# A gated mix of linear attention and a ReLU layer on one core: the kernel without its Block, a work unit on another PSUM bank, and two token tiles loaded as one

## The chip, the cores and the metric

The kernel runs on one core of a Trainium2 chip. The metric is the time of one execution on the device in microseconds; the median of several runs is given, less is better. A profiled execution gives a trace with every instruction of the five engines: TensorE (PE, its weight loads PEld), VectorE (DVE), ScalarE (ACT), GpSimd (POOL) and SyncE (SP), and of the DMA queues. A run's own time is longer than the span of its trace, which reaches from the first to the last instruction of the program.

## The reference

```python
x = A_x                                              # 1 x 2048 x 512, bf16
g = _sigmoid((x * gate_w).sum(-1, keepdims=True))
a = _A_ref(x, A_wqkv, A_w_phi, A_wo)
b = _B_ref(x, B_w1, B_w2)
return g * a + (1 - g) * b

# _A_ref, 32 heads of 16
q, k, v = qkv[0], qkv[1], qkv[2]                     # x @ wqkv, by head
pq = einsum("bhsd,hdf->bhsf", q, w_phi); pk = einsum("bhsd,hdf->bhsf", k, w_phi)
phi_q = concatenate([softmax(pq), softmax(-pq)]); phi_k = concatenate([softmax(pk), softmax(-pk)])
kv = einsum("bhsf,bhsd->bhfd", phi_k, v); z = einsum("bhsf->bhf", phi_k)
o = (phi_q @ kv) / (phi_q @ z + 1e-6)
return o.transpose(0, 2, 1, 3).reshape(B, S, D) @ wo

# _B_ref, hidden size 1376
return relu(x @ w1) @ w2
```

Each output row depends on its own token, and on all tokens only through the sums `kv` and `z`. The order in which tokens stand in the core does not matter as long as each row goes back to its place.

## The kernel before

The 2048 tokens are 16 tiles of 128 (m = 0 to 15) and four chunks of 512 (c = 0 to 3). Everything works on the transposed input XT (features by tokens) and is written out as a graph of named tasks. `ORDER` gives for each engine the order of its tasks by hand; `emit` walks it, puts a wait on a semaphore ahead of each task whose inputs come from another engine or a DMA, and each task raises the semaphore of its engine (each DMA its own).

The start, which the change touches:

- SP issues the loads in the order of `ORDER["sp"]`: token tile 0 (x00), the first and third part of W1 (w1a0, w1a2), token tiles 2 and 3 (x02, x03), the next 512 columns of W1 (w1b), w_phi (wphi), the transposing load of the keys' weights (wkT), the rest of W1 (w1c), the values' weights (wv), and the later ones. ScalarE issues x01, w1a1 and w1a3. Each of the loads x00 to x03 has 128 rows of 1 KB.
- TensorE first runs six matmuls without inputs (`warm0`, L258), then transposes the four tiles of chunk 0 by matmuls against an identity: xt{m}{n} (L350), two blocks each, n = 0, 1; the evictions into XT are xe{m}0 on ScalarE (L362) and xe{m}1 on VectorE (L365). Tile m uses the PSUM banks 0 and 1 (m = 0, 2) or 6 and 7 (m = 1, 3). The first four W1 units run in pieces as tiles and weights come in: hh0 to hh3 (L410), hr0, hr1 and h0_0 to h0_3 (L416), in banks 3, 4, 5 and 2.
- From the fifth unit on, h{c}_{k} is a W1 unit of four 512-column matmuls (L396) for chunk c and hidden tile k. It takes banks 3, 4, 5 in turn and waits until the ReLU that last read the bank, rl{c}_{k} on ScalarE (L474), is done. So h0_4 takes bank 3 after rl0_0, h0_5 bank 4, h0_6 bank 5, h0_7 bank 3 after rl0_4.
- The folds f1_0 to f1_3 (L374) multiply the keys' weights by w_phi in banks 0, 1, 6 and 7, once wkT is there. They are evicted by fe1_0 and fe1_2 on VectorE and fe1_1 and fe1_3 on ScalarE (L344, L342). The first key projection pr_k0 (L510) waits for all four.

Then follow, interleaved by `ORDER`, the W1 units, the values (L490), the key and query features (projections L510, evictions L537, maximum and minimum L541 and L543, subtractions L550, exponential L555, sums L557, normalizations L564 and L587), the sums kv (L571), their product with the queries (L614), and the two output products in one PSUM bank (L636 and L642). oe{m} on ScalarE scales and evicts a tile of the output (L687) and st{m} stores it, 128 rows of 1 KB (L690). The last tile is split by columns (L657, L668), evicted by ScalarE and VectorE and stored by both queues (L681).

At the end SP waits for the stores that nothing else waits for (L707 to L710). All five programs stand in one `nc.Block()`. With it each engine branches into its part and back, and behind it all engines meet: each drains and reports, GpSimd gathers the reports and releases them (the rows of L188). The same meeting stands ahead of the kernel, behind GpSimd's setting of some constants (the rows of L740).

Of the kernel before, what the change touches and what calls it, by code (L numbers as in the profile page):

```python
# [15 lines left out]

ORDER = {
# [4 lines left out]
    ),  # L22
# [5 lines left out]
    ),  # L28
    "act": (
# [119 lines left out]
def bass_gated_mix__linear_kernel_hedgehog__dense_activation_relu__prompt_kernel(  # L149
# [13 lines left out]
    S, D = x2.shape  # L163
# [24 lines left out]
    with ExitStack() as es:  # L188
# [43 lines left out]
        PS = E(nc.psum_tensor("PS", [P, 8, 512], FP32))  # L232
        EPS = 8 * 512

        def ap(t, row, off, dims):
            return bass.AP(tensor=t, offset=off, ap=[[row, P]] + [list(d) for d in dims])

# [49 lines left out]
        def load_x(m, eng, lat):  # L287
            load(f"x0{m}", eng, XN[:, m, :], x0r[:, m, :], dur=0.45, lat=lat)
# [7 lines left out]
        load_w(1, "act", 3.4)  # L296
        load_w(2, "sp", 3.8)
        load_w(3, "act", 3.95)
        load_x(2, "sp", 4.0)
        load_x(3, "sp", 3.9)  # L300
        load("w1b", "sp", W1[:, :, 512:1024], w1r[:, :, 512:1024], dur=0.5, lat=5.0)
        load("wphi", "sp", WPS[:, :, :], A_w_phi.rearrange("(g hl) r c -> (hl r) g c", g=ND), dur=0.5, lat=4.9)
        load_t("wkT", WT[:, ND:2 * ND, :], A_wqkv[:, D:2 * D], (), 4.1, 2.7)
# [50 lines left out]
        for m in range(4):  # L354
            for n in range(2):
                add(f"xt{m}{n}", "pe", lambda q, m=m, n=n: pe_xt(q, m, n),
                    (f"x0{m}", "ident", f"xe{m - 2}{n}" if m > 1 else None), dur=0.2, boost=9000.0 - 10 * m)
            for n, eng in enumerate(("act", "dve")):
                xo = XT[:, 2 * n:2 * n + 2, m * P:(m + 1) * P]
                xi = PS[:, XB[m][n], 0:2 * P].rearrange("p (j t) -> p j t", j=2)  # L360
                if eng == "act":
                    add(f"xe{m}{n}", eng, lambda q, o=xo, i=xi: q.activation(o, i, ACT.Copy), (f"xt{m}{n}",), dur=0.35,  # L362
                        boost=9000.0 - 10 * m)
                else:
                    add(f"xe{m}{n}", eng, lambda q, o=xo, i=xi: q.tensor_copy(o, i), (f"xt{m}{n}",), dur=0.37,  # L365
                        boost=9000.0 - 10 * m)
# [8 lines left out]
                                start=True, stop=True)  # L375
            return last

        for j in range(ND):
            b = FB[j]
            war = [f"xe{2 + j // 2}{j % 2}"]  # L380
            add(f"f1_{j}", "pe", lambda q, j=j, b=b: pe_fold(q, 1, j, b), ("wkT", *wbd, *war), dur=0.24,
                boost=1800.0)
            evict(f"fe1_{j}", ("dve", "act")[j % 2], WP[:, 1, j, :], b, (f"f1_{j}",), boost=1800.0)
        units = []
        for c in range(NC):
            units += [("h", c, k) for k in range(KT - 1)]
# [2 lines left out]
            if c == 2:  # L389
                units += [("f", 0, j) for j in range(ND)]  # L390
        freed = {b: () for b in (*HB, 2)}
        w1of = {k: (() if k < 4 else ("w1b",) if k < 8 else ("w1c",)) for k in range(KT)}

        def pe_h(q, c, k, b):
# [50 lines left out]
            add(f"go{c}", "dve", lambda q, s4=s4: q.reciprocal(OMG[:, s4], EP[:, s4]), (f"gp{c}",), dur=0.15)  # L445

        for n, (kind, a, k) in enumerate(units):
            b = GB4[n] if n < 4 else HB[(n - 4) % len(HB)]
            if kind == "h":
                halved = n < 4  # L450
                deps = [*xof[a], *w1of[k], prev, *freed[b]]
                if k == KT - 1:
                    deps.append("gw")
                    add(f"h{a}_{k}", "pe", lambda q, a=a, b=b: pe_h_tail(q, a, b), deps, dur=0.69)
                    prev = f"h{a}_{k}"
                    hrow = psap(b * 512, [[KREM + 1, 4], [1, KREM]])
                    add(f"rl{a}_{k}", "act", lambda q, a=a, i=hrow: q.activation(
                        HR[:, a % 2, :, 0:KREM], i, ACT.Relu), (prev, f"hx{a - 2}" if a > 1 else None), dur=0.6, boost=RL)
                    add(f"hx{a}", "sp", lambda q, a=a: q.dma_start_transpose(
                        out=HT[:, KT - 1, chunk(a)].rearrange("p (n t) -> p n t", t=P),  # L460
                        in_=HR[:, a % 2, :, :].rearrange("p n k -> p (n k)")),
                        (f"rl{a}_{k}", "hpad"), dur=1.2, lat=1.6, dma=True)
                    add(f"gr{a}", "dve", lambda q, a=a, b=b: q.tensor_scalar(
                        GL[:, 4 * a:4 * a + 4], psap(b * 512 + KREM, [[KREM + 1, 4]]), GATE_LIMIT, -GATE_LIMIT,
                        ALU.min, ALU.max), (prev, f"rl{a}_{k}"), dur=0.2, boost=500.0)
                    freed[b] = (f"rl{a}_{k}", f"gr{a}")
                    gate(a)
                    continue
                add(f"h{a}_{k}", "pe", lambda q, a=a, k=k, b=b, h=halved:
                    pe_h_rest(q, k, (3 if k < 2 else 2) * P, 4 * P, k > 1) if h else pe_h(q, a, k, b),  # L470
                    deps, dur=(0.22 if k < 2 else 0.44) if halved else 0.87,
                    boost=8000.0 if n < 3 else 0.0)
                prev = f"h{a}_{k}"
                add(f"rl{a}_{k}", "act", lambda q, a=a, k=k, b=b: q.activation(  # L474
                    HT[:, k, chunk(a)], PS[:, b, :], ACT.Relu), (prev,), dur=0.6, boost=RL)
                freed[b] = (f"rl{a}_{k}",)
            else:
                deps = ["wqT", *wbd, prev, *freed[b]]
                add(f"f{a}_{k}", "pe", lambda q, a=a, k=k, b=b: pe_fold(q, a, k, b), deps, dur=0.24, boost=1000.0)
                prev = f"f{a}_{k}"  # L480
                evict(f"fe{a}_{k}", FE, WP[:, a, k, :], b, (prev,), boost=1000.0)
                freed[b] = (f"fe{a}_{k}",)


        VLAG = 4
        widths = [2] * (NT // 2 - 1) + [1, 1]
# [28 lines left out]
        for jn, (kind, tiles) in enumerate(jobs):  # L515
# [61 lines left out]
            else:  # L577
# [29 lines left out]
                for m in tiles:  # L607
# [39 lines left out]
                    if m == NT - 1:  # L647
# [40 lines left out]
                        OSB[:, m % NOS, :], PS[:, ab, :], ACT.Copy, scale=OMG[:, m:m + 1]),  # L688
                        (f"a{m}", f"go{m // 4}", f"st{m - NOS}" if m >= NOS else None), dur=0.69)
                    add(f"st{m}", "act", lambda q, m=m: q.dma_start(  # L690
                        out=o2[m * P:(m + 1) * P, :], in_=OSB[:, m % NOS, :]), (f"oe{m}",), dur=0.5, lat=1.5, dma=True)

        for then in ("mx_k0", "mn_k0"):
            g.follow("mk", then)
# [3 lines left out]
        for t in g.tasks.values():  # L698
            if t.dma:
                sems[t.sem] = nc.alloc_semaphore(f"d_{t.name}")  # L700
        block = E(nc.Block())

        @block.sync
        def _(q):
            g.emit("sp", q, order, sems)

            for m in range(NT - NOS - 2, NT - 1):  # L707
                q.wait_ge(sems[f"st{m}"], 16)
            for hf in range(2):
                q.wait_ge(sems[f"st{NT - 1}_{hf}"], 16)  # L710

        @block.gpsimd
        def _(q):
            g.emit("pool", q, order, sems)

        @block.scalar
        def _(q):
            g.emit("act", q, order, sems)

        @block.vector  # L720
        def _(q):
            g.emit("dve", q, order, sems)

        @block.tensor
        def _(q):
            g.emit("pe", q, order, sems)


# [26 lines left out]
```

## Time and profile before

| | us |
|---|---|
| median of three runs | 151.93 (151.83 to 152.18) |
| the profiled execution, own time | 150.82 |
| its span in the trace | 148.9 |
| TensorE busy in it | 144.6 (97%) |
| first key projection starts (pr_k0) | 12.34 |
| last matmuls (L668) | 145.25, for 1.04 |

In timeline rows the first number is the start in us from the span's start, the second the length, then engine, line, operation, output<-input and count; rows of equal kind are merged, and in brackets stands how long the engine was idle before the row and what ended it. An engine's name with a q is its sequencer, where waits, branches and DMA issues run. Matmuls overlap: a 512-column one has a length of 379 ns, while the next begins 0.22 us after it. Some matmul records are missing from a trace.

### The profile page before, as it was taken

The page shows a single profiled execution, that of the slowest core. Times are in us where ns is not written, and L with a number is a line of the kernel's source. Part 1 is how long each engine was busy: PE and PEld are TensorE (multiplying, and loading weights), DVE is VectorE, ACT ScalarE, POOL GpSimd, SP SyncE. Part 2 cuts the span into 40 slices and gives each one's busy share as a digit, 9 for nine tenths or more (in the row PEclk, how much of TensorE's full clock was granted, in tenths as well). Part 3 has the DMA queues.
Part 4 walks back from the last instruction along what each step waited for, and adds up shares of the span by engine and source line. Part 5 has one row for each costly group of instructions (what it writes and reads, how often), then busy time and mean ns, then how long its engine had stood idle before and what let it go on. Part 6 is the DMA issues. An engine that isn't in the chain of part 4 may idle for free.

```text
span 148.9 us, 2614 instructions
## 1 busy us (share of the span) xinstructions
PE 144.6 (97%) x992; PEld 75.3 (51%) x1009; DVE 111.0 (74%) x168; ACT 91.9 (62%) x127; POOL 109.6 (74%) x72
## 2 busy tenths in 40 slices
PE   7999999999999999999999999999999999999992
PEld 2874444445654475445444554455544454455461
DVE  2532667999896948989999997999999969436301
ACT  3457769799969767898983927366565551310151
POOL 4000599999999999999999999999999791240000
DMA  4999999920030001000000191649677585966552
GB/s 149 302 205 190 220 215 193 349 71 4 12 61 0 0 4 37 0 4 0 0 0 0 36 147 35 141 106 142 153 160 198 128 213 106 143 171 146 51 167 69
DMA packets 46364, 16.11 MB, mean 108 GB/s; under 512 B 39856, under 2 KB 46352, under 8 KB 46352
## 3 DMA queue, kind: packets, MB, share of 16 engines
q1 hardware_dynamic: 43616, 13.50, 43.5%
q10 hardware_dynamic: 2736, 2.45, 5.3%
q8 instruction: 8, 0.13, 0.4%
q14 instruction: 4, 0.03, 0.1%
HBM read 4.41 MB, written 2.10 MB: 44 GB/s over the span
## 4 chain that ended last, share of the span: by engine, by line
PE 96%; ACT 1%; issue 1%; DVE 0%
PE PS L636 24%; PE PS L396 21%; PE PS L510 18%; PE PS L490 9%; PE PS L642 9%; PE PS L571 3%; PE PS L614 3%; PE PS L404 2%; PE PS L258 2%; PE PS L657 2%; PE PS L410 1%; PE PS L374 1%; PE PS L350 1%; ACT HT L474 1%; PE PS L668 1%
## 5 line engine op out<-in xcount | busy, mean ns | idle before, releaser
L550 POOL TENSOR_TENSOR TS<-PB,MX 128x1024 bf16<-128x1024 bf16 (+1 forms) x18 | 30.9, 1722 | 14.3 <-DVE MX L541 14.3
L557 DVE TENSOR_REDUCE ZB<-FT 128x128 f32<-128x2048 bf16 (+1 forms) x18 | 36.6, 2032 | 1.8 <-ACT FT L555 1.8
L636 PE MATMUL PS<-W,HT 128*128 128x512 bf16 (+1 forms) x160 | 37.5, 379 | 0.3
L555 ACT ACTIVATE FT<-TS 128x2048 bf16<-128x2048 bf16 (+1 forms) x18 | 30.9, 1718 | 8.7 <-POOL TS L550 8.5
L396 PE MATMUL PS<-XT,W 128*128 128x512 bf16 x141 | 34.3, 379 | 0.2
L550 POOL TENSOR_TENSOR TS<-MN,PB 128x1024 bf16<-128x1024 bf16 (+1 forms) x18 | 30.9, 1724 | 0.8 <-DVE MN L543 0.8
L510 PE MATMUL PS<-WP,XT 128*128 128x512 bf16 x124 | 29.9, 379 | 0.2
L564 POOL TENSOR_TENSOR FT<-FT,SC 128x2048 bf16<-128x2048 bf16 (+1 forms) x9 | 29.5, 3288 | 0.0
L474 ACT ACTIVATE HT<-PS 128x512 bf16<-128x512 f32 x40 | 22.6, 597 | 5.5 <-PE PS L396 4.6
L636 PEld LDWEIGHTS PS<-W,HT 128*128 128x128 bf16 (+1 forms) x165 | 15.5, 98 | 17.1
L541 DVE TENSOR_REDUCE MX<-PB 128x64 bf16<-128x1024 bf16 (+1 forms) x18 | 19.5, 1085 | 6.0 <-ACT PB L537 6.0
L687 ACT ACTIVATE OSB<-PS,OMG 128x512 bf16<-128x512 f32 x15 | 10.2, 687 | 22.3 <-PE PS L642 22.2
L543 DVE TENSOR_REDUCE MN<-PB 128x64 bf16<-128x1024 bf16 (+1 forms) x18 | 19.3, 1084 | 3.2 <-ACT PB L537 3.2
L396 PEld LDWEIGHTS PS<-XT,W 128*128 128x128 bf16 x144 | 13.8, 98 | 15.3
L537 ACT ACTIVATE PB<-PS 128x1024 bf16<-128x1024 f32 (+1 forms) x18 | 16.7, 927 | 6.8 <-PE PS L510 3.7
L510 PEld LDWEIGHTS PS<-WP,XT 128*128 128x128 bf16 x128 | 12.0, 98 | 13.6 <-DVE WP L344 0.4
L587 POOL TENSOR_TENSOR FT<-FT,SR 128x1024 bf16<-128x1024 bf16 (+1 forms) x9 | 15.6, 1739 | 0.7
L490 PE MATMUL PS<-WV,XT 128*128 128x512 bf16 x61 | 15.8, 379 | 0.2
L642 PE MATMUL PS<-WO,OT 128*128 128x512 bf16 x58 | 14.3, 379 | 0.1
L623 DVE SCALAR_TENSOR_TENSOR OTM<-PS,EG,RD 128x256 bf16<-128x256 f32 x32 | 13.8, 463 | 0.4 <-DVE RD L621 0.2
L621 DVE RECIPROCAL RD<-PS 128x16 f32<-128x16 f32 x32 | 6.4, 232 | 8.9 <-PE PS L614 8.7
L499 ACT ACTIVATE VS<-PS 128x512 bf16<-128x512 f32 x16 | 9.6, 602 | 4.3 <-PE PS L490 4.3
(54 smaller groups left out, 104.9 us busy)
## 6 DMA issues: line engine op xcount, KB each, us to landing
out_dram<-OSB ACTq DMA_DIRECT2D x15, 128.0 KB, 2.1
W<-in_B_w_dram SPq DMA_DIRECT2D x1, 1280.0 KB, 7.0
W<-in_B_w_dram SPq DMA_DIRECT2D x1, 512.0 KB, 5.1
WV<-in_A_wqkv_dram SPq DMA_DIRECT2D x1, 512.0 KB, 4.5
WO<-in_A_wo_dram SPq DMA_DIRECT2D x1, 512.0 KB, 7.4
FT<-in_A_x_dram SPq DMA_DIRECT2D x3, 128.0 KB, 3.7
W<-in_B_w_dram SPq DMA_DIRECT2D x1, 352.0 KB, 3.7
W<-in_B_w_dram ACTq DMA_DIRECT2D x2, 128.0 KB, 3.5
```

What stands on the lines that cost most here:

```text
L396: last = q.matmul(PS[:, b, :], W1[:, j, k * P:(k + 1) * P], XT[:, j, chunk(c)], start=(j == 0), stop=(j == ND - 1))
L474: add(f"rl{a}_{k}", "act", lambda q, a=a, k=k, b=b: q.activation(HT[:, k, chunk(a)], PS[:, b, :], ACT.Relu), (prev,), dur=0.6, boost=RL)
L490: last = q.matmul(PS[:, 2, :], XT[:, j, m * P:(m + 1) * P], WV[:, j, :], start=(j == 0), stop=(j == ND - 1))
L510: last = q.matmul(PS[:, n, :], XT[:, j, m * P:(m + 1) * P], WP[:, s, j, :], start=(j == 0), stop=(j == ND - 1))
L541: add(f"mx_{J}", "dve", lambda q, sl=sl, w=w, i=pbg: q.tensor_reduce(MX[:, sl, 0:w * H], i, AX.X, ALU.max), (f"ev_{J}", old("t1")), dur=0. ...
L543: add(f"mn_{J}", "dve", lambda q, sl=sl, w=w, i=pbg: q.tensor_reduce(MN[:, sl, 0:w * H], i, AX.X, ALU.min), (f"ev_{J}", old("t2")), dur=0. ...
L550: add(f"{tn}_{J}", "pool", lambda q, o3=o3, a3=a3, b3=b3: q.tensor_tensor(o3, a3, b3, ALU.subtract), (f"{'mx' if sg == 0 else 'mn'}_{J}", ...
L555: add(f"ex_{J}", "act", lambda q, fs=fs, ts=ts, w=w: q.activation(FT[:, fs, 0:w * F], TS[:, ts, 0:w * F], ACT.Exp), (f"t1_{J}", f"t2_{J}", ...
L557: add(f"sm_{J}", "dve", lambda q, fs=fs, sl=sl, w=w: q.tensor_reduce(ZB[:, sl, 0:2 * w * H], FT[:, fs, 0:w * F].rearrange("p (g d) -> p g ...
L564: add(f"nm_{J}", "pool", lambda q, f3=f3, sl=sl, w=w: q.tensor_tensor(f3, f3, SC[:, sl, 0:2 * w * H].unsqueeze(2).to_broadcast([P, 2 * w * ...
L636: last = q.matmul(PS[:, ab, :], HT[0:r, k, m * P:(m + 1) * P], W2[0:r, k, :], start=(k == 0), stop=False)
L642: last = q.matmul(PS[:, ab, :], OT[:, m % NOT, t, :], WO[:, t, :], start=False, stop=(t == ND - 1))
```

## The change

- The Block goes: the five programs are emitted one after the other into the main program, and SP's last waits stand behind them. No branches and no meeting of the engines remain at the end; the one ahead of the kernel stays.
- The loads x02 and x03 become one load x0b: partition p gets the rows 256+2p and 257+2p of x, which lie behind each other in memory, as one packet of 2 KB. So tile 2 holds the even and tile 3 the odd rows of the 256. All eight transposes of the two tiles wait for x0b. Their output rows go back to every second row (`stored`).
- h0_4 takes bank 6 (FB[2]) instead of bank 3 and so waits for xe30, the eviction of tile 3's first half from this bank, and not for rl0_0. f1_2, which uses bank 6 next, waits for rl0_4 as well as for xe30 (written xe{2 + j // 2}{j % 2}). h0_7 in bank 3 then waits for rl0_0.
- ScalarE does rl0_4 ahead of fe1_1 and fe1_3 instead of behind them and rl0_5.

TensorE's order and VectorE's and GpSimd's are as before.

```diff
 "sp":
-        "x00 w1a0 w1a2 x02 x03 w1b wphi wkT w1c wv x1 x2 wqT x3 ...
+        "x00 w1a0 w1a2 x0b w1b wphi wkT w1c wv x1 x2 wqT x3 ...
 "act":
-        "x01 w1a1 w1a3 xe00 xe10 xe20 xe30 rl0_0 rl0_1 rl0_3 rl0_2 fe1_1 fe1_3 rl0_5 rl0_4 ev_k0 rl0_8 rl0_6 "
+        "x01 w1a1 w1a3 xe00 xe10 xe20 xe30 rl0_0 rl0_1 rl0_3 rl0_2 rl0_4 fe1_1 fe1_3 rl0_5 ev_k0 rl0_8 rl0_6 "
...
+        def stored(m):
+            if m in (2, 3):
+                return o2[2 * P:4 * P, :].rearrange("(p n) d -> p n d", n=2)[:, m - 2, :]
+            return o2[m * P:(m + 1) * P, :]
...
-        load_x(2, "sp", 4.0)
-        load_x(3, "sp", 3.9)
+        load("x0b", "sp", FT[:, NF - 2, 2 * D:4 * D], x2[2 * P:4 * P, :].rearrange("(p m) d -> p (m d)", m=2),
+             dur=0.45, lat=3.9)
...
             add(f"xt{m}{n}", "pe", lambda q, m=m, n=n: pe_xt(q, m, n),
-                    (f"x0{m}", "ident", f"xe{m - 2}{n}" if m > 1 else None), dur=0.2, boost=9000.0 - 10 * m)
+                    (f"x0{m}" if m < 2 else "x0b", "ident", f"xe{m - 2}{n}" if m > 1 else None), dur=0.2, boost=9000.0 - 10 * m)
...
+        freed[FB[2]] = ("xe30",)
...
-            b = GB4[n] if n < 4 else HB[(n - 4) % len(HB)]
+            b = GB4[n] if n < 4 else FB[2] if n == 4 else HB[(n - 4) % len(HB)]
...
+            war = [f"xe{2 + j // 2}{j % 2}"] + (["rl0_4"] if j == 2 else [])
...
-                        out=o2[m * P:(m + 1) * P, :], in_=OSB[:, m % NOS, :]), (f"oe{m}",), dur=0.5, lat=1.5, dma=True)
+                        out=stored(m), in_=OSB[:, m % NOS, :]), (f"oe{m}",), dur=0.5, lat=1.5, dma=True)
...
-        block = E(nc.Block())
-
-        @block.sync
-        def _(q):
-            g.emit("sp", q, order, sems)
...
+        for e, q in (("sp", nc.sync), ("pool", nc.gpsimd), ("act", nc.scalar), ("dve", nc.vector), ("pe", nc.tensor)):
+            g.emit(e, q, order, sems)
+
+        for m in range(NT - NOS - 2, NT - 1):
+            nc.sync.wait_ge(sems[f"st{m}"], 16)
+        for hf in range(2):
+            nc.sync.wait_ge(sems[f"st{NT - 1}_{hf}"], 16)
```

More of the change, by code (lines that the diff above doesn't have):

```diff
@@ L376, in pe_fold @@
             return last
[L378 to L383, printed above, removed]
         units = []
@@ L482, in bass_gated_mix__linear_kernel_hedgehog__dense_activation_relu__prompt_kernel @@
                 freed[b] = (f"fe{a}_{k}",)
+        for j in range(ND):
+            b = FB[j]
+            war = [f"xe{2 + j // 2}{j % 2}"] + (["rl0_4"] if j == 2 else [])
+            add(f"f1_{j}", "pe", lambda q, j=j, b=b: pe_fold(q, 1, j, b), ("wkT", *wbd, *war), dur=0.24,
+                boost=1800.0)
+            evict(f"fe1_{j}", ("dve", "act")[j % 2], WP[:, 1, j, :], b, (f"f1_{j}",), boost=1800.0)
         VLAG = 4
@@ L700, in bass_gated_mix__linear_kernel_hedgehog__dense_activation_relu__prompt_kernel @@
                 sems[t.sem] = nc.alloc_semaphore(f"d_{t.name}")
-        block = E(nc.Block())
-        @block.sync
-        def _(q):
-            g.emit("sp", q, order, sems)
[L707 to L726, printed above, removed]
+        for e, q in (("sp", nc.sync), ("pool", nc.gpsimd), ("act", nc.scalar), ("dve", nc.vector), ("pe", nc.tensor)):
[4 more added lines that the diff above has]
+            nc.sync.wait_ge(sems[f"st{NT - 1}_{hf}"], 16)
 _INS = ['A_x', 'A_wqkv', 'A_w_phi', 'A_wo', 'B_x', 'B_w1', 'B_w2', 'gate_w']
```

2 rows, old and new, of the table ORDER are left out of this document.

## The prediction

> **What bounds the kernel now.** I read the page first, then the chain that ended last, then the stages and the start and the end instruction by instruction.
>
> ```profile
> span 148.9 us, 2614 instructions
> PE 144.6 (97%) x992; PEld 75.3 (51%) x1009; DVE 111.0 (74%) x168; ACT 91.9 (62%) x127; POOL 109.6 (74%) x72
> PE 96%; ACT 1%; issue 1%; DVE 0%
> ```
>
> The third line is the chain by engine: from the first matmul to the last the time is TensorE's. The table by stage says where TensorE is not simply busy (stretch, length, then busy time and instructions of PE, PEld, DVE, ACT, POOL, clock, DMA):
>
> ```profile
> 12.34:143.00 130.66, 129.81 (x872) 65.70 (x888) 105.33 (x152) 83.85 (x113) 107.92 (x63) 1.00 0.47 97
> 146.32:148.90 2.58, 0.00 (x0) 0.00 (x0) 0.38 (x1) 0.28 (x1) 0.00 (x0) 1.00 0.17 51
> ```
>
> Between 12.34 and 143 TensorE has 0.85 us without a record in 130.66, at clock 1.00. No instruction of that stretch changes, so it can only move as a block. The change can act before 12.34, where loads still decide, and after 146.32, where 2.58 us pass with no matmul.
>
> **The start, as it is.** TensorE's rows around token tiles 2 and 3 and the fifth W1 unit (start, length):
>
> ```profile
> 5.63 0.38 PE L410 MATMUL PS<-XT,W 128*128 128x256 bf16 x2
> 5.95 0.23 PEld L350 LDWEIGHTS PS<-IDN,FT 128*128 128x128 bf16 x4 [0.21 <-DMA FT<-in_A_x_dram]
> 6.30 0.23 PEld L350 LDWEIGHTS PS<-IDN,FT 128*128 128x128 bf16 x4
> 6.54 0.60 PE L410 MATMUL PS<-XT,W 128*128 128x256 bf16 x4
> 8.63 0.42 PEld L396 LDWEIGHTS PS<-XT,W 128*128 128x128 bf16 x3
> 8.96 1.67 PE L396 MATMUL PS<-XT,W 128*128 128x512 bf16 x7
> ```
>
> Four 256-column matmuls take 0.60 of which the last 0.27 is its own length, so they start 0.11 apart; the one before the wait starts at 5.63+0.11=5.74 and leaves TensorE free at 5.85. It goes on at 5.95 (load x02, 0.10 lost), does four transposes in 0.23, and goes on again at 6.30 (load x03, 0.12 lost). The rest of the start runs without a gap until 8.96.
>
> There the chain of waits leaves TensorE for ScalarE:
>
> ```profile
> 7.84 1.09 ACT HT L474 x2
> ```
>
> That would be the fifth unit, h0_4, waiting for rl0_0 to free bank 3. It is a missing record (the page has 992 matmuls to 1009 weight loads): two units are eight matmuls and seven are shown, while the weight loads begin at 8.63 and go on one matmul ahead. 8.96 is the second matmul of h0_4, 0.22 after an unrecorded one at 8.74. h0_4 does not wait for a bank.
>
> **Part 1: the Block goes.** At the end (one row per instruction: duration three times, then first and last start):
>
> ```profile
> L710 SPq EVENT_SEMAPHORE  x2: 28/28/28, 148.3 to 148.5; - x2
> L188 PEldq DRAIN  x1: 1757/1757/1757, 144.6 to 144.6; - x1
> L188 SPq COMPARE_BRANCH  x1: 33/33/33, 148.6 to 148.6; - x1
> L188 SPq DRAIN  x1: 7/7/7, 148.7 to 148.7; - x1
> L188 POOLq EVENT_SEMAPHORE  x2: 17/17/17, 148.8 to 148.8; - x2
> L188 PEldq EVENT_SEMAPHORE  x1: 51/51/51, 148.9 to 148.9; - x1
> ```
>
> SP's wait for the last store ends at 148.5. Then come a branch, a drain, GpSimd's gathering and release, and every engine's passing of it, until 148.9: 0.4 us in series behind the last store, and nothing hides it. All of it goes, so the span ends with the wait at 148.5: **-0.4 us**. The other drains lie under SP's wait already and give nothing.
>
> Outside the span lie 150.82-148.9=1.9 us of the profiled run. No row shows them. Today all engines leave the kernel together at 148.9; then the other four would leave before SP, TensorE by 4 us (its drain at 144.6), and closing work that they must do one after another could lie under SP's wait. The nearest rows for how far apart engines come when no barrier holds them are the opening ones:
>
> ```profile
> L740 SPq DRAIN  x1: 7/7/7, 0.0 to 0.0; - x1
> ...
> L740 PEldq DRAIN  x1: 8/8/8, 0.3 to 0.3; - x1
> ...
> L740 SPq EVENT_SEMAPHORE  x1: 17/17/17, 0.7 to 0.7; - x1
> ```
>
> ```profile
> 0.74 0.40 SPq L272 DMA_DIRECT2D FT<-in_A_x_dram  x1
> ...
> 2.13 0.91 SPq L272 DMA_DIRECT2D FT<-in_A_x_dram  x2
> ```
>
> 0.3 us between the first and the last. Bounds 0 and -0.3; a loss I exclude, since no engine arrives later than today. I take the middle, **-0.15**. At the entry the branches have no row; between SP's release (0.7 above) and its first load (0.74, in SP's timeline) lie some 0.05 us, so they cost between 0 and 0.05: **-0.03**, and it shifts loads and warm-up matmuls alike.
>
> **Part 2: x02 and x03 become x0b.** From the page the queues (packets, MB, share of 16 engines' span) and the landings (count, KB each, us from issue to landing):
>
> ```profile
> q1 hardware_dynamic: 43616, 13.50, 43.5%
> q10 hardware_dynamic: 2736, 2.45, 5.3%
> ...
> W<-in_B_w_dram SPq DMA_DIRECT2D x1, 512.0 KB, 5.1
> ...
> FT<-in_A_x_dram SPq DMA_DIRECT2D x3, 128.0 KB, 3.7
> ```
>
> x0b is issued at 2.13 (SP's timeline above), where x02 was. Its first half is no longer usable before its second. How long do 2 KB packets take? q10: 5.3% of 16x148.9 us over 2736 packets is 46 ns for 895 bytes on the mean; q1: 43.5% over 43616 is 23.8 ns for 310 bytes. That is 0.038 ns a byte and 12 ns a packet: estimated 51 ns for 1 KB and 90 for 2 KB. Each of 16 engines moves 8 of the 128 packets: 8x(2x51-90)=0.10 us saved. So I let x0b release TensorE 0.10 before x03 did, at 6.20. Eight transposes take 2x0.235=0.47 (four and the step to the next group are 6.54-6.30=0.24), the next matmuls (hh3) start at 6.67 instead of 6.54: **+0.13**. Even is a release at 6.07.
>
> The rule that speaks against the joining is in the Trainium skill, "DMA: Bandwidth & Descriptors", section "Why a DMA increments its semaphore by 16 and not by 1": only the full 16, one from each engine, means that the data is there. The trace agrees (two loads, two releases, 5.95 and 6.30); by it the joined load costs tile 2 the 0.25 between 5.95 and my 6.20.
>
> Bounds of the release: not before TensorE is free at 5.85, -0.22 (both gaps); and by size between the 3.7 us of 128 KB and the 5.1 us of 512 KB, a third of the way up, 4.2 us: landing at 6.3, release 6.4, +0.33. I take +0.13, nearest x03's own row, since the same engines move the same bytes.
>
> The evictions of both tiles come right behind:
>
> ```profile
> 6.27 0.74 ACT L362 ACTIVATE XT<-PS 128x256 bf16<-128x256 f32 x2 [1.61 <-PE PS L350]
> 6.38 0.78 DVE L365 CAST XT<-PS 128x256 bf16<-128x256 f32 x2 [1.47 <-PE PS L350]
> 6.97 1.93 PE L416 MATMUL PS<-XT,W 128*128 128x128 bf16 x24
> ```
>
> VectorE's first cast (half of the 0.78 and a little, 0.43) ends at 6.81, 0.86 after the first transpose. TensorE wants it at 6.97 now, 1.02 after; without the pause between the tiles it comes 0.47+0.43=0.90 after, with its weight load a little sooner: 0 to 0.05, **+0.02**.
>
> SP issues one load fewer, some 0.45 us; w1b, wphi and wkT are issued that much sooner. That buys nothing as long as TensorE comes later than before. The stride of tiles 2 and 3 on the way out keeps 128 rows of 1 KB, and
>
> ```profile
> ACT OSB L687 <- PE PS L642: 22.2, 12, 8.3
> ```
>
> the evictions behind those stores wait 22.2 us for TensorE, not for stores: 0. Uncovered, a store's landing of 2 us would stand before an eviction.
>
> **Part 3: h0_4 to bank 6.** It loses a wait on rl0_0 that was over (above): 0. In exchange f1_2 waits for rl0_4, which ScalarE now does ahead of fe1_1:
>
> ```profile
> 7.84 2.18 ACT L474 ACTIVATE HT<-PS 128x512 bf16<-128x512 f32 x4 [0.83 <-PE PS L416]
> 10.37 0.98 PEld L374 LDWEIGHTS PS<-WBD,WT 128*128 128x128 bf16 x16 [0.23 <-DMA WT<-in_A_wqkv_dram]
> 11.12 1.08 ACT L342 ACTIVATE WP<-PS 128x512 bf16<-128x512 f32 x2 [1.09 <-PE PS L374]
> 12.31 0.13 PEld L510 LDWEIGHTS PS<-WP,XT 128*128 128x128 bf16 x2 [0.42 <-DVE WP L344]
> ```
>
> ScalarE is done with four rl at 10.02; a fifth of 0.6 ends at 10.6. f1_2 loads half-way through 0.98 from 10.37, at 10.86, and fe1_1 starts at 11.12: it fits in ScalarE's 1.09 idle with 0.26 to spare, and all of it shifts with TensorE. Cost 0; were rl0_4 later by x, f1_2, f1_3, fe1_2 and pr_k0 (12.31) would be later by x-0.26.
>
> **Sum:** -0.4-0.15-0.03+0.13+0.02 = -0.43 us; the profiled run's 150.82 becomes 150.4. The three timed runs have a median of 151.93, 1.1 above the profiled run; I carry the difference over: **151.5 us**.
>
> **The rivals.**
> - *The front gains as well.* x0b releases before 5.85, and the 0.22 of gaps goes. For it: one issue and half the packets. Against: the 128 KB loads took 3.7 us at this place, queued behind 768 KB. wkT then stops part of it: the fold's weight load waited until 10.37 with a matmul slot at 10.47, so 0.1 passes unless wkT comes earlier too, which its earlier issue speaks for. Price: 151.93-0.58-0.22=151.1. The Trainium skill's same page, "Anatomy of one DMA", has a fit (for the other, software path) of 2.0 us plus bytes over 436 GB/s: 2.6 us for 256 KB, a landing at 4.7 and this result. For 128 KB it gives 2.3, and the rows say 3.7, so I do not believe it here.
> - *The end gains nothing.* What follows the span joins the engines at the same hour anyway, and only the front is left: 151.93+0.15-0.03=152.05. For it: 1.9 us outside the span that I cannot see. Against: the last store is SP's alone to wait for, and the 0.4 lies in series behind it. That is the case in which the change doesn't do what it says.
> - *Slower: x0b is late.* One slow DMA engine holds all eight transposes, where today tile 2 can go ahead. At the 512 KB load's 5.1 us it would land at 7.23; hh3 starts at 7.75, 1.2 later, and 151.93-0.58+1.2=152.55. It decides from a release of 6.07+0.58=6.65 on. Against: twice the bytes of x02, not four times.
>
> **How the numbers follow.** A change of 0.2% is 0.30 us, about what can be told from none, so 151.63 to 152.23 is "no change". The forecast 0.58, the front gaining 0.14, the end not gaining 0.18, x0b late 0.10. The forecast's own bounds are 150.95 (-0.4-0.3-0.05-0.22) and 151.9 (-0.4+0.38); some 0.05 of its chance lies above 151.63. Faster 0.53+0.14=0.67; no change 0.05+0.17=0.22; slower 0.11. Range 150.95 to 152.05: it takes in the gaining front and the end that gains nothing, and leaves out the late load and the outermost corners.
>
> **What would show it.** The span's last row is SP's wait, with no branch, drain or gathering behind it, and the time outside the span is 1.6 to 1.9 us. One group of eight transposes starts near 6.2 with one wait, hh3 near 6.65. h0_4's weight loads follow on without a gap and the fold shows no wait for ScalarE. The stretch from the first pr_k0 matmul to the last keeps its 130.7 us. Wrong it is if x0b's release lies outside 5.85 to 6.5, if the time outside the span grows by what the span loses, or if waits on ScalarE or GpSimd appear between 13 and 143.

## The result, and the profile after

| | before | changed |
|---|---|---|
| median of 22 runs each, us | 151.55 (150.74 to 152.40) | 150.99 (150.33 to 151.67) |
| the profiled execution, own time | 150.82 | 151.05 |
| its span | 148.9 | 149.4 |
| time outside the span, mean over the runs (before: its 86 runs beside the experiments) | 1.86 | 1.61 |

The ratio is 0.9962, 95% interval 0.9947 to 0.9977: the change makes the kernel 0.56 us faster, about 0.4%. A second comparison of the same two kernels (e5 below) gave 150.91 beside 151.18, ratio 0.9978 (0.9958 to 0.9998). Two of its twelve runs, 152.77 and 152.98, were in a slower state and are left out here and below. Forecast was -0.43 us.

The two profiled executions tell the opposite at first sight, since the span after is 0.5 us *longer*. The page and the table by stage of the changed kernel:

```profile
span 149.4 us, 2618 instructions
PE 145.6 (97%) x1009; PEld 74.9 (50%) x1009; DVE 110.8 (74%) x168; ACT 91.7 (61%) x127; POOL 109.5 (73%) x72
...
12.34:143.00 130.66, 130.66 (x888) 65.36 (x885) 106.05 (x154) 84.03 (x114) 107.87 (x63) 1.00 0.46 97
```

This time no matmul record is missing (1009 to 1009 weight loads), and TensorE is busy through all of 12.34 to 143: the 0.85 us without a record before were missing records and no wait. The difference lies at the two edges. First the end; the group of SP's last waits of the changed kernel (last two numbers: first and last start):

```profile
L714 SPq EVENT_SEMAPHORE  x2: 28/28/28, 149.2 to 149.4; - x2
```

It is the last row of the span. The branch, the drain and the gathering that followed it for 0.4 us before are gone. Now the start, TensorE's weight loads in the timeline of the changed kernel:

```profile
4.99 0.21 PEld L410 LDWEIGHTS PS<-XT,W 128*128 128x128 bf16 x2
6.20 0.34 PEld L410 LDWEIGHTS PS<-XT,W 128*128 128x128 bf16 x4 [1.01 <-issue]
6.84 0.45 PEld L355 LDWEIGHTS PS<-IDN,FT 128*128 128x128 bf16 x8 [0.29 <-DMA FT<-in_A_x_dram]
7.25 0.37 PEld L410 LDWEIGHTS PS<-XT,W 128*128 128x128 bf16 x4
7.82 1.67 PEld L416 LDWEIGHTS PS<-XT,W 128*128 128x128 bf16 x24 [0.20 <-ACT XT L367]
9.51 1.50 PEld L396 LDWEIGHTS PS<-XT,W 128*128 128x128 bf16 x8
11.13 1.10 PEld L379 LDWEIGHTS PS<-WBD,WT 128*128 128x128 bf16 x16
12.18 0.58 PEld L396 LDWEIGHTS PS<-XT,W 128*128 128x128 bf16 x4
13.19 0.13 PEld L517 LDWEIGHTS PS<-WP,XT 128*128 128x128 bf16 x2 [0.42 <-DVE WP L349]
```

All eight transposes stand in one group with one wait, as forecast, but at 6.84 and not at 6.20, and ahead of them TensorE waits 1.01 us. What it waits for there is in the waits of the changed kernel (us in total, times, longest):

```profile
PE PS L410 <- DMA W<-in_B_w_dram: 0.8, 1, 0.8
```

A quarter of W1 (w1a2, which hh2 needs ahead of tile 2) was late: it landed 4.4 us after its issue, and 3.3 us before. The change does not touch this load. That the larger packets behind it hold it up is not shown: it took 3.6 to 4.4 us in the six profiles with the joined load, and 3.3 to 4.4 in the seven with two loads. pr_k0 starts at 13.19, 0.88 after the 12.31 of before, and the end gives 0.4 back: that is the longer span. Is 0.9 us the price of the joined load? One execution can't say: the spans of the changed kernel's runs alone reach from 148.7 to 150.0 us. The experiments show that this start was an unlucky one, and that of the profile before a lucky one. The start makes most of the spread: from pr_k0's first weight load to the span's end pass 136.1 to 136.4 us in every profile without the Block.

### The profile page after: what moved, and what is told of

Same layout as the page of the kernel before. It is cut to its first block, busy times and chain, and to the rows that moved or that the text cites. A ratio compares the mean times of both kernels' runs of the same rounds, so it can differ in the third digit from the quotient of the medians.

```text
span 149.4 us, 2618 instructions
## 1 busy us (share of the span) xinstructions
PE 145.6 (97%) x1009; PEld 74.9 (50%) x1009; DVE 110.8 (74%) x168; ACT 91.7 (61%) x127; POOL 109.5 (73%) x72
## 4 chain that ended last, share of the span: by engine, by line
PE 94%; DMA 3%; SPq 1%; DVE 0%; issue 0%
PE PS L643 24%; PE PS L396 21%; PE PS L517 19%; PE PS L497 9%; PE PS L649 9%; DMA W<-in_B_w_dram 3%; PE PS L578 3%; PE PS L621 3%; PE PS L404 2%; PE PS L664 2%; PE PS L416 1%; PE PS L379 1%; PE PS L410 1%; PE PS L675 1%; SPq L277 1%; PE PS L355 0%
## 5 line engine op out<-in xcount | busy, mean ns | idle before, releaser
L643 PE MATMUL PS<-W,HT 128*128 128x512 bf16 (+1 forms) x165 | 38.1, 379 | 0.0
L517 PE MATMUL PS<-WP,XT 128*128 128x512 bf16 x128 | 30.6, 379 | 0.0
L497 PE MATMUL PS<-WV,XT 128*128 128x512 bf16 x64 | 16.4, 379 | 0.0
```

Source lines behind the costliest of these rows:

```text
L497: last = q.matmul(PS[:, 2, :], XT[:, j, m * P:(m + 1) * P], WV[:, j, :], start=(j == 0), stop=(j == ND - 1))
L517: last = q.matmul(PS[:, n, :], XT[:, j, m * P:(m + 1) * P], WP[:, s, j, :], start=(j == 0), stop=(j == ND - 1))
L643: last = q.matmul(PS[:, ab, :], HT[0:r, k, m * P:(m + 1) * P], W2[0:r, k, :], start=(k == 0), stop=False)
```

## The experiments

Each kernel was timed beside runs of the kernel before, in lots: e1 to e4 (median before 151.47), e5 to e8 (151.18), e9 to e11 (151.22), e12 (151.39). In the table "span" is the mean span less that of the lot's runs of before, with its 95% bound; "outside" is the mean of time less span; tile 2 and pr_k0 are the starts of their first weight load in the one profiled execution. Kernel before: outside 1.84 to 1.89, tile 2 5.95, pr_k0 12.31.

| | what it is | median | ratio, 95% | span | outside | tile 2 | pr_k0 |
|---|---|---|---|---|---|---|---|
| e1 | no Block alone | 150.25 | 0.9926, 0.9897 to 0.9955 | -0.65±0.33 | 1.33 | 6.29 | 12.71 |
| e6 | the same again | 150.25 | 0.9946, 0.9926 to 0.9966 | -0.35±0.26 | 1.33 | 6.50 | 13.07 |
| e2 | joined load alone | 151.30 | 0.9988, 0.9971 to 1.0005 | -0.22±0.17 | 1.85 | 6.46 | 13.03 |
| e3 | bank and order alone | 151.38 | 0.9988, 0.9972 to 1.0004 | -0.15±0.20 | 1.84 | 6.61 | 13.05 |
| e4 | no Block, bank, order | 150.45 | 0.9935, 0.9910 to 0.9959 | -0.50±0.26 | 1.32 | 6.28 | 12.70 |
| e5 | changed kernel again | 150.91 | 0.9978, 0.9958 to 0.9998 | -0.09±0.23 | 1.61 | 6.71 | 13.05 |
| e7 | e1, waiting for both loads | 150.78 | 0.9971, 0.9947 to 0.9996 | -0.03±0.29 | 1.37 | 6.98 | 13.34 |
| e8 | changed, rl0_4 late | 151.86 | 1.0044, 1.0024 to 1.0065 | +0.87±0.23 | 1.60 | 6.39 | 14.04 |
| e10 | changed, one wait more | 150.49 | 0.9949, 0.9929 to 0.9969 | -0.22±0.22 | 1.33 | 6.55 | 12.89 |
| e11 | e1, permuted rows | 150.31 | 0.9931, 0.9909 to 0.9953 | -0.37±0.30 | 1.35 | 6.43 | 13.25 |
| e12 | changed, two waits more | 150.57 | 0.9948, 0.9922 to 0.9973 | -0.27±0.30 | 1.32 | 6.43 | 12.87 |

### e1 and e6: only the Block goes

```diff
-        block = E(nc.Block())
-        @block.sync
...
+        for e, q in (("sp", nc.sync), ("pool", nc.gpsimd), ("act", nc.scalar), ("dve", nc.vector), ("pe", nc.tensor)):
+            g.emit(e, q, order, sems)
+        for m in range(NT - NOS - 2, NT - 1):
+            nc.sync.wait_ge(sems[f"st{m}"], 16)
```

> The kernel before with nothing changed but the Block taken away. Forecast of the prediction: -0.4 us in the span, about -0.15 outside it (the first chip result suggests up to -0.27: 1.92 us lay outside the span before, 1.65 after), nothing at the entry: -0.55 to -0.7 us, a ratio of 0.9955 to 0.9965. Rival 'only what the span shows': -0.4 us, 0.9973, with 1.9 us outside the span. Rival 'the end gains nothing': 1.000, the span shorter and the time outside it longer by the same 0.4.

> The kernel without the Block alone, as the partner of the run above: 0.992 to 0.994 against before. Span some 0.45 us shorter than before's, time outside it some 0.5 us shorter. If the -0.5 outside the span belonged to one chip only, it falls to the 0.3 of the first result: 0.995.

Both lots gave 150.25 us, 1.2 and 0.9 us below their runs of before, and about 0.7 below the changed kernel. From the last weight load on TensorE to the span's end pass 2.53 us in e1 and 2.93 to 2.96 in the kernels with the Block; the last row is SP's wait again:

```profile
L707 SPq EVENT_SEMAPHORE  x2: 28/28/28, 148.6 to 148.8; - x2
```

That is the 0.4 us inside the span. Outside it the kernel gains a further 0.53 us (1.86 to 1.33), three and a half times what the prediction gave it and twice what the changed kernel has. The gain forecast for e1 (0.9955 to 0.9965) was too small for that reason. So the changed kernel loses half of that gain again, and something in its start too.

### e2: only the joined load

```diff
-        load_x(2, "sp", 4.0)
-        load_x(3, "sp", 3.9)
+        load("x0b", "sp", FT[:, NF - 2, 2 * D:4 * D], x2[2 * P:4 * P, :].rearrange("(p m) d -> p (m d)", m=2),
```

> The kernel before with x02 and x03 joined to x0b, Block and banks as before. Forecast: +0.13 to +0.15 us, 1.001. Rival 'the front gains as well': -0.22 us, 0.9985. Rival 'the joined load is late': +0.5 us and more, 1.003 or above. In the trace one wait ahead of eight transposes.

No difference in time that the runs can tell: 0.9988, and 1.85 us outside, as before. The forecast of 1.001 lies just outside the interval, and the value is nearer to the rival in which the front gains (0.9985): the mean span is 0.22 us shorter, not longer. With the Block the joined load costs nothing outside the span. In its profile:

```profile
6.46 0.45 PEld L355 LDWEIGHTS PS<-IDN,FT 128*128 128x128 bf16 x8 [0.61 <-DMA FT<-in_A_x_dram]
...
11.16 0.90 PEld L379 LDWEIGHTS PS<-WBD,WT 128*128 128x128 bf16 x16 [0.54 <-DMA WT<-in_A_wqkv_dram]
```

The transposes waited 0.61 us for x0b, and the folds waited for wkT, although SP had issued wkT sooner than before. The earlier issue of the later loads bought nothing.

### e3 and e4: the bank and ScalarE's order, with the Block and without

```diff
+        freed[FB[2]] = ("xe30",)
-            b = GB4[n] if n < 4 else HB[(n - 4) % len(HB)]
+            b = GB4[n] if n < 4 else FB[2] if n == 4 else HB[(n - 4) % len(HB)]
-            war = [f"xe{2 + j // 2}{j % 2}"]
+            war = [f"xe{2 + j // 2}{j % 2}"] + (["rl0_4"] if j == 2 else [])
```

> The kernel before with h0_4 in bank 6 and rl0_4 ahead of fe1_1, nothing else. Forecast: 0, ratio 1.000, since h0_4 waited for nothing and ScalarE has 0.26 us to spare for f1_2. Rival 'the 1.1 us on ScalarE in the chain is a wait': -0.2 us or more, 0.9985 or below. Rival 'the fold waits for rl0_4': +0.2 us or more, and a wait for ScalarE at TensorE's L379 or its like.

> The changed kernel with the two loads x02 and x03 of before. If the joined load costs 0.13 us: 0.13 us less than the changed kernel, -0.7 us against before, 0.9953. If it gains 0.22: 0.22 more than the changed kernel, -0.36, 0.9976. If the parts add up, the same as without the Block alone.

0.9988 alone, and without the Block 0.9935 beside the 0.9926 and 0.9946 of e1 and e6: the moved bank gains and costs nothing that can be measured.

### e5, e7: the changed kernel again, and two loads that are both awaited

```diff
-                    (f"x0{m}", "ident", f"xe{m - 2}{n}" if m > 1 else None), dur=0.2, boost=9000.0 - 10 * m)
+                    (*((f"x0{m}",) if m < 2 else ("x02", "x03")), "ident", f"xe{m - 2}{n}" if m > 1 else None), ...
```

> The changed kernel once more, beside the kernel without the Block alone on the same chip. The first comparisons leave 0.4 us between the two (0.9962 and 0.9926), with 1.61 us outside the span for the one and 1.33 for the other, though the rows behind the last store are alike. If that is the chip, both have the same time outside the span here and differ by the joined load alone: forecast +0.13 us against no Block, that is 0.994 to 0.9955 against before. Rival 'the joined load costs more without the Block': 0.996 again, 0.4 us behind.

> No Block; x02 and x03 stay two loads of 1 KB packets, but all eight transposes wait for both. It takes the joint waiting without the 2 KB packets. If the joint waiting is what costs and the packets give 0.10 us back: +0.23 us against no Block alone, +0.10 against the changed kernel. Rival 'the packets give nothing': the same as the changed kernel. Rival 'the wait is on w1a2 and w1a3 anyway, ahead of it': the same as no Block alone.

e5 and e6 ran on one chip, and 1.61 and 1.33 us outside the span came again: that difference belongs to the kernels and not to the chip. The forecast for e5 (0.994 to 0.9955), which took them to be equal there, missed.

e7 has no Block and the two loads of before, but no transpose of either tile begins before both are there. Beside e6 in the same lot its median is 0.5 us higher (0.9971 against 0.9946) and its mean span 0.32±0.36 us longer. That points the way of the forecast (+0.23, since tile 2 may not go ahead) but is not clear of the noise; beside the changed kernel (e5) the mean span is 0.06 us longer. Its rows:

```profile
6.98 0.46 PEld L350 LDWEIGHTS PS<-IDN,FT 128*128 128x128 bf16 x8 [0.42 <-DMA FT<-in_A_x_dram]
7.40 0.37 PEld L410 LDWEIGHTS PS<-XT,W 128*128 128x128 bf16 x4
7.97 1.68 PEld L416 LDWEIGHTS PS<-XT,W 128*128 128x128 bf16 x24 [0.20 <-ACT XT L362]
```

Here too TensorE comes to a stop behind hh3, ahead of the group of 24 (hr0 is its first), as in the changed kernel at 7.82. Which eviction does hr0 wait for? VectorE's casts, of the changed kernel and of e7:

```profile
7.28 0.76 DVE L370 CAST XT<-PS 128x256 bf16<-128x256 f32 x2 [2.45 <-PE PS L355]
```

```profile
7.43 0.76 DVE L365 CAST XT<-PS 128x256 bf16<-128x256 f32 x2 [2.62 <-PE PS L350]
```

And of e1, its weight loads and its casts:

```profile
7.34 1.68 PEld L416 LDWEIGHTS PS<-XT,W 128*128 128x128 bf16 x24
```

```profile
6.80 0.76 DVE L365 CAST XT<-PS 128x256 bf16<-128x256 f32 x2 [2.18 <-PE PS L350]
```

The group of 24 begins 7.82-7.28=0.54 us after the first cast's start here, 7.97-7.43=0.54 in e7, 7.34-6.80=0.54 in e1, and 6.93-6.38=0.55 before, where the prediction saw no wait. A distance that stays the same, whatever else moved, points to a wait, although the profile puts it down to ScalarE: 0.42 for the cast of tile 2 and 0.12 until the weight load goes; hr0 needs tile 2's two evictions alone. It is 0.54 or 0.55 in twelve of the thirteen profiles. The cast begins 0.44 after tile 2's first transpose in both kernels (7.28-6.84, 6.38-5.95). So the start hangs on **tile 2**, already before the change, and the rest follows at a fixed distance: from the group of 24 to pr_k0 it is 5.37 after and 5.38 before.

The thirteenth is e11 (two loads, below). There x03 landed late, at 7.19, and the group of 24 follows behind hh3 without a stop, 0.86 after the cast of tile 2, which began at 6.94:

```profile
7.23 0.23 PEld L356 LDWEIGHTS PS<-IDN,FT 128*128 128x128 bf16 x4 [0.51 <-DMA FT<-in_A_x_dram]
7.42 0.37 PEld L416 LDWEIGHTS PS<-XT,W 128*128 128x128 bf16 x4
7.80 1.75 PEld L422 LDWEIGHTS PS<-XT,W 128*128 128x128 bf16 x24
```

So the second of two loads can decide as well, when it is late enough. And tile 2 does not always start at its load's release. In e6 x02 landed at 5.33 and the last quarter of W1 at 5.17, yet tile 2's first transpose came at 6.50. TensorE was busy until then with the pieces of W1, at half its pace. Its L410 rows between 4.9 and 7, of the kernel before and of e6 (ns, shortest/median/longest; first and last start):

```profile
L410 PE MATMUL PS<-XT,W x17: 219/272/314, 4.6 to 6.9; 128*128 128x256 bf16 x12, 128*128 128x128 bf16 x5
```

```profile
L410 PE MATMUL PS<-XT,W x11: 314/421/421, 4.7 to 6.5; 128*128 128x256 bf16 x8, 128*128 128x128 bf16 x3
```

In e6 the 256-column matmuls start 0.21 us apart, before 0.11. e3 and e12 keep the slow pace beyond 6.0 too; in the other ten profiles it ends between 3.5 and 5.7. The granted clock shown for this stretch of e6 is 1.00, so its rows do not say why. The scatter of the start thus comes from loads and from TensorE's own early pace.

### e8: the cover of rl0_4 taken away

```diff
-  "... rl0_2 rl0_4 fe1_1 fe1_3 rl0_5 ..."
+  "... rl0_2 fe1_1 rl0_4 fe1_3 rl0_5 ..."
```

> The changed kernel with rl0_4 behind fe1_1 instead of ahead of it on ScalarE: the cover of the fold's new wait is taken away. fe1_1 starts 0.75 us after the fold's first weight load and lasts 0.5, rl0_4 another 0.6: f1_2 starts some 1.3 us later than in the changed kernel, and TensorE with it: +1.3 us, 1.005 against before. Rival 'the fold's eviction or wkT is waited for anyway': less than +0.3 us.

In the changed kernel ScalarE's rows around the fold are

```profile
8.72 2.67 ACT L474 ACTIVATE HT<-PS 128x512 bf16<-128x512 f32 x5 [0.89 <-PE PS L416]
11.99 1.08 ACT L347 ACTIVATE WP<-PS 128x512 bf16<-128x512 f32 x2 [0.60 <-PE PS L379]
```

The fifth rl ends at 11.39, and f1_2, the ninth of the sixteen weight loads from 11.13, comes at 11.73: 0.34 us to spare; 0.26 was forecast. In e8 that cover is gone:

```profile
10.67 0.65 PEld L379 LDWEIGHTS PS<-WBD,WT 128*128 128x128 bf16 x8
12.67 0.45 PEld L379 LDWEIGHTS PS<-WBD,WT 128*128 128x128 bf16 x8 [1.35 <-ACT HT L474]
...
14.04 0.34 PEld L517 LDWEIGHTS PS<-WP,XT 128*128 128x128 bf16 x3 [0.38 <-DVE WP L349]
```

TensorE waits 1.35 us for ScalarE between f1_1 and f1_2. The mean span is 0.96 us above that of e5 in the same lot and the median time 0.95; the profile alone would say 1.3 (from tile 2's first transpose to pr_k0 it is 7.65 in e8 and 6.35 in the changed kernel). The edit that costs nothing costs about a microsecond when one task stands one place later.

### e9: the loads by themselves

This kernel leaves the whole computation out and only loads and copies rows of x.

```diff
+        for r in range(8):
+            sp.dma_start(out=X[:, 2:4, :], in_=x2[2 * P:4 * P, :].rearrange("(p m) d -> p m d", m=2)).then_inc(j, 16)
+            sp.wait_ge(j, 16)
+            sp.dma_start(out=X[:, 4, :], in_=x2[4 * P:5 * P, :]).then_inc(a, 16)
+            sp.dma_start(out=X[:, 5, :], in_=x2[5 * P:6 * P, :]).then_inc(b, 16)
+            sp.wait_ge(a, 16)
+            sp.wait_ge(b, 16)
```

> This kernel leaves the whole computation out: SP loads rows of A_x and stores a copy of them, nothing else runs, so only its rows are read and not its time. Eight times it loads 256 KB of two neighbouring rows to a partition (packets of 2 KB, line 34) and waits, then loads two times 128 KB (packets of 1 KB, lines 37 and 38) and waits for both; after that come loads in bulk. Theory (the joined load costs and gains next to nothing, as the estimate of 51 ns for a 1 KB packet and 90 ns for one of 2 KB had it): the median packet of 2 KB takes 80 to 95 ns and that of 1 KB 43 to 53 ns, and the joined load is complete 0.0 to 0.3 us before the second load of the pair counted from the first issue of each, and after the first load of the pair by 0.1 to 0.5 us. Rival one (larger packets move clearly more): a 2 KB packet under 75 ns, and the joined load at least 0.4 us ahead of the pair's second. Rival two (larger packets are worse): a 2 KB packet over 105 ns, and the joined load behind the pair's second.

SP's issues in its timeline: L34 is the joined load, L37 and L38 the pair, and each group is issued when the one ahead is complete.

```profile
6.08 0.33 SPq L34 DMA_DIRECT2D X<-in_A_x_dram  x1
8.61 0.33 SPq L37 DMA_DIRECT2D X<-in_A_x_dram  x1
8.98 0.43 SPq L38 DMA_DIRECT2D X<-in_A_x_dram  x1
11.26 0.33 SPq L34 DMA_DIRECT2D X<-in_A_x_dram  x1
```

The joined load takes 8.61-6.08=2.53 us here and the pair 2.65. From the issue to the landing of the last byte the eight joined loads have a median of 2.60 and the pairs of 2.54, so they are even; the first load of a pair is there at 2.05, half a microsecond ahead of either. The median packet took 84 ns for 2 KB and 46 ns for 1 KB, near the estimates of 90 and 51, but single packets took up to 587 and 307 ns, and the means are 110 and 53. The forecast that the joined load would be a little ahead of the pair's second missed by a hair; both rivals fall on the packets. With these means the prediction's sum for the saving, 8x(2x51-90)=0.10 us, becomes 8x(2x53-110)=-0.03: the larger packets save nothing. The fit in the Trainium skill, "DMA: Bandwidth & Descriptors", section "Anatomy of one DMA", made there for the software path, gives an estimate of 2.6 us for 256 KB: the 2.60 of a load alone, as here, agree. Its estimate of 2.3 for 128 KB is above the 2.05 measured.

In the kernel, behind 768 KB, it is another matter. The page of the changed kernel (count, KB each, us from issue to landing):

```profile
FT<-in_A_x_dram SPq DMA_DIRECT2D x1, 256.0 KB, 4.7
```

### e10, e11, e12: where half of the gain outside the span went

The time outside is 1.61 us in the changed kernel and 1.33 without the Block and with two loads; with the Block it is the same with one load or two. No row shows it.

```diff
+        nc.sync.wait_ge(sems["x0b"], 16)
         for m in range(NT - NOS - 2, NT - 1):
             nc.sync.wait_ge(sems[f"st{m}"], 16)
```

> The changed kernel with one more wait in SyncE's program, ahead of the five last ones, on the joined load, which landed 130 us earlier: it waits for nothing. What is tested is the time outside the span, which is 1.33 us on the mean in the kernels without the Block and with two loads, and 1.61 us without the Block and with the joined load. Theory A (it hangs on the length or the place of SyncE's program, which is one load shorter with the joined load): with one instruction more the time outside the span comes to 1.33 us and the kernel to 150.75 us beside 151.02 of the changed kernel, ratio to before 0.996. Theory B (it hangs on the load itself, its 2 KB packets, its descriptors or the rows' order): outside stays at 1.61 us, the time within 0.2 us of 151.0 us, ratio 0.998. A span longer by more than 0.1 us on the mean would say that the met wait itself costs; about 0.05 us is forecast by both.

e11 keeps two loads and takes the rows as the changed kernel does:

```diff
+        x0p = x2[2 * P:4 * P, :].rearrange("(p n) d -> p n d", n=2)
+        for m in (2, 3):
+            load(f"x0{m}", "sp", XN[:, m, :], x0p[:, m - 2, :], dur=0.45, lat=3.9)
```

> The kernel before without the Block, with two loads for token tiles 2 and 3 as before (128 KB each, packets of 1 KB, a semaphore each), but each takes every second row of the 256, and the rows of both tiles are stored back by the same stride as in the changed kernel; bank and order of the fifth unit as before. Theory A (number of loads or of instructions): the time outside the span is 1.33 us on the mean as with two loads in plain order, and the kernel comes to 150.3 us, ratio to before 0.994. Theory B1 (the permuted rows or the strided stores make the time outside): 1.61 us outside, 150.55 us. Theory B2 (the 2 KB packets of the load alone make it): 1.33 us outside, as under A; the run with one more wait tells A from B2. For the strided stores themselves the prediction had no cost: the stretch from the last weight load on PE to the span's end stays at 2.5 us, as without the Block and with plain stores (2.51 to 2.53).

One wait more, on something that was over long ago, brings the outside to 1.33 us (1.31 to 1.35 in six runs; 1.58 to 1.68 without it) and the kernel to 150.49. Theory A is borne out, B falls: it is not the load, its packets or the rows' order, for e11 has the permuted rows and 1.35. e11 also shows the strided stores to cost nothing (2.53 us from the last weight load to the span's end, as in e1). e12 was meant to ask whether it is odd or even counts:

```diff
+        nc.sync.wait_ge(sems["x0b"], 16)
+        nc.sync.wait_ge(sems["w1b"], 16)
```

> The changed kernel with two more met waits in SyncE's program ahead of the five last ones, on the joined load and on the first W1 block behind it, both of which landed 130 us earlier. SyncE's program counts 73 instructions in the changed kernel (1.61 us outside the span), 74 with one wait more and in the kernels without the Block and with two loads (1.33 us). Theory A1 (it hangs on whether the count is odd or even, that is on where the program's end falls): with 75 instructions the time outside the span is 1.61 us again and the kernel comes to 150.8 to 151.0 us, ratio to before 0.998. Theory A2 (a length below 74 is what costs): 1.33 us outside, 150.5 us, ratio 0.995. Theory A3 (another period, such as one of four instructions): a third value, between 1.2 and 1.8 us.

1.32 us outside, as in e10. But e12 does not answer that, since SyncE's last waits stand two to an instruction. The first group of them in the changed kernel, in e10 and in e12 (the second group has two rows in each):

```profile
L712 SPq EVENT_SEMAPHORE  x2: 28/28/28, 148.0 to 148.1; - x2
```

```profile
L713 SPq EVENT_SEMAPHORE  x3: 17/28/28, 147.7 to 147.8; - x3
```

```profile
L714 SPq EVENT_SEMAPHORE  x3: 28/28/28, 147.7 to 147.8; - x3
```

e12 has as many rows as e10. Over the whole trace SyncE has 73 instructions in the changed kernel and 74 in e10, in the kernels without the Block and with two loads, and in e12 too, not the 75 of its expectation. So e12 repeats e10. Shown is that SyncE's program of 73 instructions has 1.60 to 1.61 us outside the span and each of those of 74 has 1.32 to 1.37. Whether it is the length, odd against even counts, or the place of what follows the program, stays open, and so does why: how the closing work follows a program can't be seen in a trace, and other counts without the Block weren't tried.

## Why the prediction was right, point by point

- **The end inside the span, forecast -0.4: right.** From the last weight load to the span's end 2.93 to 2.96 us with the Block, 2.51 to 2.53 without, in every profile: -0.42 on the mean. The rival in which the end gains nothing falls with e1.
- **Outside the span, forecast -0.15: too small, and for an incomplete reason.** It is -0.25 in the changed kernel and -0.53 with the Block alone gone. That the other engines leave early and closing work passes under SP's wait was argued from the opening rows and bounded at -0.3; e1 goes beyond that bound, and no run tests the reason. (TensorE would leave some 2.6 us early and not 4: its drain starts at 144.6 but lasts 1.757 us.) And the prediction took this term for one that only the Block decides, while one instruction in SyncE's program moves it by 0.28 us. So it is luck that -0.15 lies near -0.25: the Block alone gave 0.38 more than forecast, and the shorter program, of which the prediction knew nothing, took 0.28 of it back.
- **The entry, forecast -0.03: nothing.** SP's first load is issued at 0.74 in both.
- **The front, forecast +0.13 and +0.02: the size fits what was measured, which is not much; the step was wrong for the profile it was read from.** The prediction let x03's release set the rest, so that x0b would break even at 6.07, and gave VectorE's cast 0.05 of delay because TensorE "wants it" at 6.97, 0.12 after the cast's end. But those 0.12 are the handover, and the cast was already what TensorE waited for. So break-even in that profile is x02's release, 5.95; only in e11 does x03 set the rest. That is how the quoted rule on the semaphore of 16 in the Trainium skill, "DMA: Bandwidth & Descriptors", section "Why a DMA increments its semaphore by 16 and not by 1", counted it: tile 2 pays from its own release to that of the whole. In the six profiles with two separately awaited loads (before, e1, e3, e4, e6, e11) tile 2 starts at 6.34 on the mean, in the six with the joined load (changed, e2, e5, e8, e10, e12) at 6.56: 0.22±0.23 later. pr_k0 is later by 0.16±0.3 (12.85 and 13.01, without e8). The mean spans without the Block say +0.27±0.20 (e5, e10, e12 against e1, e4, e6, e11), while e2, with the Block, has a shorter span than before. So a cost of 0.1 to 0.3 us is likely without the Block, and why e2 shows none is open.
- **The release itself, forecast 6.20 against 6.30.** It was 6.84 in the profile, outside the 5.85 to 6.5 that the prediction set itself, and by its own rule the slower rival decides from 6.65 on. It did not win, because the profile before was no fair measure: its own time of 150.82 is near the lowest of 22 runs (150.74), and its tile 2 the earliest of the thirteen profiles. The price has to be taken between means. In the six profiles with it x0b landed between 6.24 and 6.80, 6.50 on the mean; in the six with two separately awaited loads x02 landed at 5.98 and x03 at 6.42 on the mean. So x0b came about when x03 did, and the 0.10 that its larger packets were to save does not show here either.
- **The bank, forecast 0: right** (e3, e4), with the forecast cover of 0.26 us measured at 0.34 and priced by e8. **The strided stores, 0: right** (e11).
- **The sum.** -0.42, -0.25 and about +0.2 make -0.5; -0.56 was measured in the first comparison and some -0.3 (ratio 0.9978) in the second. That the time came out at 150.99 and not nearer 151.5, only 0.04 above the lower end of the range, is for the most part the level: the prediction started from the median of three runs, 151.93, and 22 runs have 151.55.

The version that beats both kernels is e1: the Block goes, and the two loads and the bank stay as they were, 150.25 us. The changed kernel with one idle wait more (150.49) comes near it.

## What to carry to other kernels

A barrier that stands in series behind the last store is worth its rows and more: look at the run's time less its span too, over many runs, for what no row shows. Joining two loads saves an issue, but the work on the first half then waits for the last byte of the whole; find which half the path hangs on, by a distance that stays the same between traces, before pricing it. Where an experiment adds an instruction, count the rows in its trace before reading the result. At such a start one profile is one throw of the dice: take starts and spans over several executions before a tenth of a microsecond is read from them.

## What was not expected of the hardware

- The time outside the span is steady to a few hundredths of a microsecond within a kernel without the Block (1.31 to 1.35 in e10, 1.58 to 1.68 in e5), but is 0.28 us longer with 73 instructions in SyncE's program than with 74.
- A packet of 2 KB took 84 ns at the median and one of 1 KB 46 ns, with the same landing for 256 KB alone in either form (2.60 and 2.54 us); single packets took up to 587 ns.
- TensorE's 256-column matmuls at the start stand 0.21 us apart in some executions until after 6.0 us and 0.11 in others, at a shown granted clock of 1.00.
- The span of the same program differs between executions by more than the whole change, 1.3 us between the shortest and the longest of the changed kernel, and for the most part by its start.
